# Second attention: the mask added by VectorE, scores in single-bank steps, and one fixed TensorE order of 270 steps

## The chip, the core and the metric

The kernel runs on one core of one Trainium2 chip. The metric is device time in microseconds (us), here that of this one core. TensorE multiplies matrices into banks of PSUM (a tile of this kernel takes one bank, 512 fp32 columns at most); VectorE (DVE in the rows) and ScalarE (ACT) read PSUM and work on SBUF; GpSimd (POOL) works on SBUF; DMA queues are issued from SyncE (SP) and GpSimd. Each engine runs its own list of instructions in order and waits on semaphores that others raise.

## The reference

Three stages run one after the other on 4 batches of 576 positions with 512 features:

```python
x = attn(q, k, v)            # 8 heads of 64; half local, half strided masks
x = moe(x, ...)              # 8 experts, one chosen per position
# second attention: 4 experts that are attention heads of 64, top 2 per position
for e in range(E):
    q, k, v = x @ wq[e], x @ wk[e], x @ wv[e]
    scores = scale * (q @ k.transpose(0, 2, 1))
    scores = np.where(causal, -1e9, scores)       # causal: key after query
    a = exp(scores - scores.max(-1)); a /= a.sum(-1) + 1e-9
    out += top2_weight(e) * (a @ v @ wo[e])
```

The change concerns the third stage alone.

## The kernel before, in words

The second attention holds, per batch, the 4 experts as two pairs (`pr` 0 and 1) of two heads (`h`). Its work is cut into steps, each a Python function that issues instructions for several engines:

- `c_load`/`c_t`: load 128 positions of the second stage's output and transpose them on TensorE; ScalarE and VectorE split the result into a high and a low part (`split`, L106 to L108).
- `c_qk`: 12 matmuls of 288 columns (tile `qkp`, three per product, `mm3` at L110 to L113); ScalarE and VectorE then make the halves of `qkt` (L1160, L1161 and `split`). `c_v`: 12 matmuls of 260 columns (`vp`).
- `c_s`: one **unit** of scores, that is one pair and one block `i` of queries (0 to 4; keys 64, 192, 320, 448 or 576). For blocks 0 and 1 both heads share one PSUM bank (tile `cs`), for 2 and 3 each head has one, for 4 each head has two of 288 keys. Of a pair's 10 banks 8 end on the diagonal, 64 in the stage. In such a bank a bf16 matmul against an identity (L1225, `idb` as weights, `mc` as data, 128 columns for one head, 2 x 64 or 2 x 128 for two) first writes the mask, then two fp32r matmuls per head add the scores (L1230). VectorE takes the row maximum (L1232), ScalarE the exponential and its sum (L1234), VectorE the reciprocal and weight (L1250 to L1252, or L1240 to L1247 for block 4), both engines scale the rows (L1257, L1259), and GpSimd clears 64 columns behind them (L1260). Tile `E` has 3 buffers; the banks of `cs` come in turn from three (`rot`, L95: two of tag `s`, one of `et`).
- `c_et`: transposes of one head's scaled scores (tile `cet`, two banks, L1274 and L1279), copied to SBUF by ScalarE or VectorE (L102, L104).
- `c_pv`: the product with the values for 256 or 320 queries (tile `cpv`, L1304): 4 or 10 matmuls in plain fp32, two records each. The two heads use the two halves of TensorE's columns.
- `c_out`: 6 matmuls of 512 columns (`cop`), a ScalarE copy and the DMA out.

`c_qk`, `c_v`, `c_pv`, `c_out` and, from batch 1 on, `c_t` take three banks in turn (`misc`, L96: `xt`, `lg`, `pv`).

Each step has a due time (tables `TAB`; a unit is 2 apart from the next), the steps are issued in the order of these times (L1382), and the framework's scheduler then sets every engine's list, moving instructions of different steps past and between each other. This is so for TensorE too: in the second attention nothing fixes its order by hand (the second stage does, `tc.manual_schedule`).

## Time and profile before

| what | value |
|---|---|
| median of 3 runs | 608.93 us (606.72 to 610.8) |
| the profiled execution: own time | 608.12 us |
| its span, first to last instruction | 606.3 us |
| TensorE busy, share of the span | 95% |
| VectorE, ScalarE, GpSimd | 61%, 58%, 24% |
| second attention on TensorE | first transpose at 386.96 us, last matmul at 601.39 us |

How to read it: matmuls are pipelined, so a matmul's duration in the rows (0.29 us for 288 columns) is longer than the time it costs in a row of such matmuls (0.13 us from start to start). What a matmul costs is therefore read here from the start of one to the start of the next. In the timeline rows, instructions of one line and shape that follow each other stand as one row with their count.

### The profile page before, as it was taken

How to read it: one execution, taken by the hardware profiler on the slowest of the kernel's cores; microseconds unless marked ns; L12 is line 12 of the kernel's file. 1: busy time of each engine (PE TensorE's matmuls, PEld its weight loads, DVE VectorE, ACT ScalarE, POOL GpSimd, SP SyncE). 2: the span in 40 equal slices, each digit the busy share in tenths (PEclk: the TensorE clock that was granted, in tenths of full speed). 3: DMA queues.
4: the chain of work that ended last, by engine and by line, in shares of the span. 5: the costliest groups of instructions: out<-in, count | busy, mean ns of one | idle time of the engine just before them, and what ended most of it. 6: DMA issues, size and time to landing. Idle time of an engine off the chain costs nothing. (4 is left out here: it accounts for less than half of the span.)

```text
span 606.3 us, 14268 instructions
## 1 busy us (share of the span) xinstructions
PE 578.4 (95%) x5329; PEld 493.5 (81%) x5329; DVE 371.8 (61%) x1071; ACT 349.9 (58%) x868; POOL 147.9 (24%) x229
## 2 busy tenths in 40 slices
PE   7898999889899999999999999999999999999996
PEld 4786788678688998989898977898888897988764
DVE  3456788936565563554646564358877686867671
ACT  2565767531555554445555665338677676847782
POOL 8242323421333423343343543200000000000000
PEclk9699799979999999999999999999999999999999
DMA  9999889440695472566566510424015102211202
GB/s 181 175 243 261 211 204 257 129 131 23 216 325 160 163 219 96 193 241 211 169 190 179 172 60 14 147 64 126 1 41 136 61 12 58 82 54 40 75 37 86
DMA packets 81219, 82.47 MB, mean 136 GB/s; under 512 B 56808, under 2 KB 56808, under 8 KB 80624
## 3 DMA queue, kind: packets, MB, share of 16 engines
q1 hardware_dynamic: 73024, 65.58, 39.0%
q0 software_dynamic: 8112, 15.76, 7.9%
q8 instruction: 55, 0.90, 0.6%
q14 instruction: 28, 0.23, 0.1%
HBM read 62.42 MB, written 21.76 MB: 139 GB/s over the span
## 5 line engine op out<-in xcount | busy, mean ns | idle before, releaser
L185 POOL DMA_INDIRECT yd<-y,sidx x47 | 54.1, 1150 | 81.9 <-ACT y L951 52.3
L108 DVE TENSOR_TENSOR w1l<-w1raw,w1h 128x1024 fp32r<-128x1024 f32 (+1 forms) x44 | 42.2, 982 | 30.5 <-ACT w1h L107 30.5
L1260 POOL MEMSET E<- 128x128 f32 x40 | 8.2, 207 | 188.4 <-PE cet L1279 93.9
L111 PE MATMUL yp<-w2h,h 128*128 128x512 f32 x128 | 52.8, 412 | 0.4 <-ACTq L961 0.4
L1234 ACT ACTIVATE E<-cs,c_mx 128x288 f32<-128x288 f32 (+4 forms) x96 | 45.9, 483 | 9.1 <-DVE c_mx L1232 4.8
L107 ACT ACTIVATE w1h<-w1raw 128x1024 fp32r<-128x1024 f32 (+1 forms) x44 | 34.4, 833 | 28.6 <-PE hp L113 18.5
L113 PE MATMUL yp<-w2h,h 128*128 128x512 f32 x128 | 50.3, 393 | 0.0
L112 PE MATMUL yp<-w2l,h 128*128 128x512 f32 x128 | 49.9, 390 | 0.0
L108 DVE TENSOR_TENSOR w2l<-w2raw,w2h 128x512 fp32r<-128x512 f32 x56 | 35.6, 684 | 11.6 <-ACT w2h L107 5.4
L1230 PE MATMUL cs<-qkt 128*128 128x288 f32 (+4 forms) x192 | 41.9, 331 | 0.0
L1232 DVE TENSOR_REDUCE c_mx<-cs 128x1 f32<-128x288 f32 (+4 forms) x80 | 37.8, 484 | 2.9 <-PE cs L1230 2.2
L111 PE MATMUL qkp<-y,cw 128*128 128x288 f32 x128 | 39.1, 305 | 0.4 <-DVE y L108 0.4
L113 PE MATMUL qkp<-y,cw 128*128 128x288 f32 x128 | 37.8, 296 | 0.0
L112 PE MATMUL qkp<-y,cw 128*128 128x288 f32 x128 | 37.8, 296 | 0.0
L107 ACT ACTIVATE w2h<-w2raw 128x512 fp32r<-128x512 f32 x56 | 32.3, 632 | 9.0 <-PE yp L113 4.5
L694 DVE SCALAR_TENSOR_TENSOR h<-hp,h 128x384 fp32r<-128x384 f32 x48 | 24.9, 550 | 14.5 <-ACT h L693 14.5
L951 ACT ACTIVATE y<-yp,pslot 128x512 f32<-128x512 f32 x22 | 14.9, 683 | 31.5 <-PE yp L113 22.9
L111 PE MATMUL hp<-xo,w1h 128*128 128x320 f32 (+1 forms) x96 | 31.7, 331 | 0.0
L179 POOL DMA_INDIRECT xg<-xd,gidx x24 | 24.4, 1016 | 27.8 <-DVE gidx L637 20.8
L111 PE MATMUL hp<-xh,w1h 128*128 128x384 f32 (+2 forms) x96 | 30.8, 321 | 0.0
L112 PE MATMUL hp<-xo,w1h 128*128 128x320 f32 (+1 forms) x96 | 30.6, 319 | 0.0
L113 PE MATMUL hp<-xo,w1l 128*128 128x320 f32 (+1 forms) x96 | 30.6, 318 | 0.0
(365 smaller groups left out, 1730.8 us busy)
## 6 DMA issues: line engine op xcount, KB each, us to landing
w1raw<-in_moe_w_dram SPq DMA_DIRECT2D x32, 512.0 KB
w2raw<-in_moe_w_dram SPq DMA_DIRECT2D x56, 256.0 KB
yr<-yd SPq DMA_DIRECT2D x20, 256.0 KB
qkt<-qkt SPq DMA_DIRECT2D x8, 576.0 KB
out_dram<-co SPq DMA_DIRECT2D x16, 256.0 KB
raw<-in_q_dram SPq DMA_DIRECT2D x16, 144.0 KB
raw<-in_k_dram SPq DMA_DIRECT2D x16, 144.0 KB
raw<-in_q_dram SPq DMA_DIRECT2D x8, 288.0 KB
```

The source lines that it names most:

```text
L107: nc.scalar.activation(hi, src, AF.Copy)
L108: (eng or nc.vector).tensor_tensor(lo, src, hi.bitcast(FT), op=OP.subtract)
L111: nc.tensor.matmul(o, ah, bh, start=start, stop=False, **kw)
L112: nc.tensor.matmul(o, ah, bl, start=False, stop=False, **kw)
L113: nc.tensor.matmul(o, al, bh, start=False, stop=stop, **kw)
L179: nc.gpsimd.indirect_dma_start(out=t, out_offset=None, in_=xd[:rows], in_offset=bass.IndirectOffsetOnAxis(ap=gidx[:, r, e:e + 1], axis=0))
L185: nc.gpsimd.indirect_dma_start(out=yds[n], out_offset=bass.IndirectOffsetOnAxis(ap=ix(n), axis=0), in_=y, in_offset=None, bounds_check=yds ...
L694: nc.vector.scalar_tensor_tensor(lo, p, 0.0, hi.bitcast(FT), op0=OP.max, op1=OP.subtract)
L951: nc.scalar.activation(y, p, AF.Copy, scale=pslot[:, r, e:e + 1])
L1230: nc.tensor.matmul(o[:, h - h0], T[:, h, q0:q0 + PQ], T[:, 2 + 2 * x + h, k0:k1], start=x == 0 and not last, stop=x == 1, skip_group_check ...
L1232: nc.vector.tensor_reduce(mx[:PQ, n, h0:h0 + G], o, axis=AX.X, op=OP.max, negate=True)
L1234: nc.scalar.activation(E[:PQ, h, k0:k1], o[:, h - h0], AF.Exp, bias=mx[:PQ, n, h:h + 1], accum_out=sm[:PQ, n, h:h + 1])
```

## The change

`c_s` is cut into one step for each PSUM bank of scores (`groups`); the mask matmul is gone, and in its place VectorE adds the bf16 mask `mc` in PSUM, onto the 128 (or 2 x 64, 2 x 128) diagonal columns of a finished bank, before it takes the maximum. Tiles, buffers, banks and all other instructions stay as they are, and so does the choice of engine for every copy. The 270 steps are sorted by due time as before, then put into the order of a table `ORD2`, and `manual_schedule` makes TensorE's list follow it; the lists of the other engines are still set by the scheduler.

```diff
+ORD2 = [0, 17, 7, 2, 3, 1, 8, 4, 6, 5, 9, 11, 10, 12, 13, 20, 14, 16, 15, 19, 18, 22, 24, 21, 26, 23, 30, 36, 27, 32,
...
-    def c_s(g):
+    def groups(i):
+        nk = NS[i + 1]
+        if nk <= 256:
+            return [(0, 0, nk, 0, 2)]
+        parts = [(0, nk)] if nk <= 512 else [(0, 288), (288, nk)]
+        return [(n, k0, k1, h, 1) for n, (k0, k1) in enumerate(parts) for h in range(2)]
+
+    def c_s(g, j):
...
+        n, k0, k1, h0, G = gs[j]
+        last = k1 == nk
+        p = cbank("cs", [128, G, 512 // G], "cs")
+        o = p[:, :, :k1 - k0]
+        for h in range(h0, h0 + G):
+            for x in range(2):
+                nc.tensor.matmul(o[:, h - h0], T[:, h, q0:q0 + 128], T[:, 2 + 2 * x + h, k0:k1],
+                                 start=x == 0, stop=x == 1, skip_group_check=True)
+        if last:
+            d = p[:, :, q0 - k0:k1 - k0]
+            nc.vector.tensor_tensor(d, d, mc[:, None, :P].to_broadcast([128, G, P]), op=OP.add)
+        nc.vector.tensor_reduce(mx[:, n, h0:h0 + G], o, axis=AX.X, op=OP.max, negate=True)
...
-                if last:
-                    nc.tensor.matmul(p[:PQ, :, q0 - k0:k1 - k0], idb[:PQ, :PQ],
-                                     mc[:PQ, None, :P].to_broadcast([PQ, G, P]), start=True, stop=False,
-                                     skip_group_check=True)
...
-    for _, f, a in sorted(ev, key=lambda x: x[0]):
+    ev.sort(key=lambda x: x[0])
+    cctx.enter_context(tc.manual_schedule(engines={mybir.EngineType.PE}))
+    for i in ORD2 or range(len(ev)):
+        _, f, a = ev[i]
         f(*a)
```

On TensorE, at the seam between batch 0 and batch 1 (`cpv` is the product with the values, `cs` the scores, `cet` the transposes, `qkp` and `cop` the projections). Before:

```order
L1304 MATMUL cpv<-et,vz_7194 64x320
L1230 MATMUL cs<-qkt 128x64 x4
L1230 MATMUL cs<-qkt 128x192 x4
L1304 MATMUL cpv<-et,vz_7194 64x320 x5
L1304 MATMUL cpv<-et,vz_7194 64x192 x2
L1304 MATMUL cpv<-et,vz_7194 64x64 x2
L1279 MATMUL cet<-idf,E 128x128
L1304 MATMUL cpv<-et,vz_7194 64x256
L1279 MATMUL cet<-idf,E 128x128
L1304 MATMUL cpv<-et,vz_7194 64x256
L1304 MATMUL cpv<-et,vz_7194 64x128 x2
```

The same two products after the change:

```order
L1241 MATMUL cs<-qkt 128x64 x4
L1297 MATMUL cet<-idf,E 128x128 x2
L1322 MATMUL cpv<-et,vz_7194 64x320 x6
L1322 MATMUL cpv<-et,vz_7194 64x192 x2
L1322 MATMUL cpv<-et,vz_7194 64x64 x2
L1241 MATMUL cs<-qkt 128x192 x4
```

```order
L1322 MATMUL cpv<-et,vz_7194 64x256 x2
L1322 MATMUL cpv<-et,vz_7194 64x128 x2
```

Each product with the values had been cut in two, its first matmul ahead of other work; now each runs in one piece (between the two pieces shown stand six matmuls of `cop`). Over the whole stage the 16 products stood in 23 pieces and now stand in 15, one of them two products long.

On TensorE, batch 0, pair 1, block 2. Before, with the mask's weights and matmul ahead of each head's scores:

```order
L1274 MATMUL cet<-idf,E 128x128
L1279 MATMUL cet<-idf,E 128x128
L1225 LDWEIGHTS idb
L1225 MATMUL cs<-mc,idb 128x128
L1230 MATMUL cs<-qkt 128x320 x2
L1225 LDWEIGHTS idb
L1225 MATMUL cs<-mc,idb 128x128
L1230 MATMUL cs<-qkt 128x320 x2
```

After the change the same block's scores, with those of block 0 behind them:

```order
L1241 MATMUL cs<-qkt 128x320 x4
L1241 MATMUL cs<-qkt 128x64 x4
L1292 MATMUL cet<-idf,E 128x128 x3
L1297 MATMUL cet<-idf,E 128x128
L1292 MATMUL cet<-idf,E 128x128 x3
L1297 MATMUL cet<-idf,E 128x128
```

All 64 mask matmuls with their weight loads are gone from TensorE's list (three of them had been moved ahead, into the end of the second stage).

On VectorE, at the last two units of the last batch (`c_mx` the maxima, `c_sm`, `c_rw` the sums and weights, `et` copies of transposes). Before:

```order
L1232 TENSOR_REDUCE c_mx<-cs 128x1
L108 TENSOR_TENSOR ot_9871<-cpv,ot_9870 128x256
L1252 TENSOR_TENSOR c_rw<-c_sm,t_w 128x2
L1232 TENSOR_REDUCE c_mx<-cs 128x1
L108 TENSOR_TENSOR ott<-cpv,ott 128x64
L1259 TENSOR_SCALAR E<-E,c_rw 128x448
L1232 TENSOR_REDUCE c_mx<-cs 128x1 x2
```

After:

```order
L1246 TENSOR_REDUCE c_mx<-cs 128x1
L1269 RECIPROCAL c_sm<-c_sm 128x2
L1245 TENSOR_TENSOR cs<-cs,mc 128x128
L1270 TENSOR_TENSOR c_rw<-c_sm,t_w 128x2
L1246 TENSOR_REDUCE c_mx<-cs 128x1
L1277 TENSOR_SCALAR E<-E,c_rw 128x448
L1245 TENSOR_TENSOR cs<-cs,mc 128x128
L1246 TENSOR_REDUCE c_mx<-cs 128x1
L119 TENSOR_TENSOR ot_9882<-cpv,ot_9881 128x256
```

Each of the 64 adds (L1245) stands ahead of its bank's maximum, with at most a few instructions of other steps between.

## Rows read from the trace of the kernel before

**Rows 1.** The page, clock granted to TensorE in 40 slices, tenths of full.

```profile
PEclk9699799979999999999999999999999999999999
```

**Rows 2.** Windows: length, busy us of PE, PEld, DVE, ACT, POOL, clock, DMA.

```profile
400.20:452.20 52.00, 50.46 (x395) 46.23 (x394) 41.45 (x156) 35.33 (x116) 1.90 (x9) 1.00 0.23 58
452.20:504.20 52.00, 51.37 (x381) 44.80 (x380) 37.78 (x137) 35.47 (x116) 2.05 (x10) 1.00 0.26 69
504.20:556.20 52.00, 52.00 (x383) 45.62 (x382) 36.54 (x135) 35.42 (x114) 1.85 (x9) 1.00 0.22 59
```

**Rows 3.** Groups by form, 391 to 606 us, mask matmuls: busy, mean ns.

```profile
L1225 PE MATMUL cs<-mc,idb 128*128 128x128 bf16 x54 | 12.2, 226 | 0.1
...
L1225 PE MATMUL cs<-mc,idb 128*128 128x256 bf16 x7 | 2.0, 279 | 0.0
```

**Rows 4.** Timeline of TensorE, block 2's scores: start us, length us, what, count.

```profile
441.37 0.22 PE L1225 MATMUL cs<-mc,idb 128*128 128x128 bf16 x1
...
441.78 0.23 PE L1225 MATMUL cs<-mc,idb 128*128 128x128 bf16 x1
...
442.19 0.29 PE L111 MATMUL qkp<-y,cw 128*128 128x288 f32 x1
442.32 0.29 PE L112 MATMUL qkp<-y,cw 128*128 128x288 f32 x1
```

**Rows 5.** Timeline of TensorE, a long product with the values in one piece.

```profile
432.09 0.27 PE L1279 MATMUL cet<-idf,E 128*128 128x128 f32 x1
432.29 2.28 PE L1304 MATMUL cpv<-et,vz 128*64 128x320 f32 x20
434.50 0.66 PE L1274 MATMUL cet<-idf,E 128*128 128x128 f32 x4
```

**Rows 6.** Timeline of TensorE, a short product in one piece.

```profile
576.97 0.87 PE L1304 MATMUL cpv<-et,vz 128*64 128x256 f32 x8
577.77 0.66 PE L1274 MATMUL cet<-idf,E 128*128 128x128 f32 x4
```

**Rows 7.** Timeline of TensorE, two products in two pieces each.

```profile
451.66 0.29 PE L113 MATMUL qkp<-y,cw 128*128 128x288 f32 x1
451.89 0.75 PE L1304 MATMUL cpv<-et,vz 128*64 128x320 f32 x2
452.57 1.14 PE L1230 MATMUL cs<-qkt 128*128 128x64 f32 x8
453.63 2.27 PE L1304 MATMUL cpv<-et,vz 128*64 128x320 f32 x18
455.83 0.33 PE L1279 MATMUL cet<-idf,E 128*128 128x128 f32 x1
456.09 0.65 PE L1304 MATMUL cpv<-et,vz 128*64 128x256 f32 x2
456.67 0.33 PE L1279 MATMUL cet<-idf,E 128*128 128x128 f32 x1
456.94 0.86 PE L1304 MATMUL cpv<-et,vz 128*64 128x256 f32 x6
457.74 0.40 PE L111 MATMUL qkp<-y,cw 128*128 128x288 f32 x1
```

**Rows 8.** Waits of TensorE, 391 to 606 us: total us, times, longest.

```profile
PE cet L1279 <- POOL E L1260: 1.3, 2, 0.6
PE cet L1279 <- DVE c_sm L1251: 1.0, 1, 1.0
```

**Rows 9.** Groups by form, VectorE, operations on a PSUM tile: busy, mean ns.

```profile
L108 DVE TENSOR_TENSOR ot<-cpv,ot 128x256 fp32r<-128x256 f32 x16 | 6.7, 420 | 7.7 <-ACT ot L107 7.7
...
L108 DVE TENSOR_TENSOR ott<-cpv,ott 128x64 fp32r<-128x64 f32 x8 | 1.7, 218 | 0.4 <-ACT ott L107 0.3
```

**Rows 10.** Timeline of TensorE, the last scores and their transposes.

```profile
586.66 0.51 PE L1230 MATMUL cs<-qkt 128*128 128x288 f32 x2
...
591.82 0.60 PE L1274 MATMUL cet<-idf,E 128*128 128x128 f32 x4
```

## The prediction

> **What bounds the kernel now.** I read the page first for the clock: TensorE had the full clock from the tenth of 40 slices on, all through the second attention [rows 1]; nothing is to be won or lost there unless long gaps appear. Then the windows view, cut at the repeating pattern of the batches, which is 52.0 us long: TensorE is busy 50.5, 51.4 and 52.0 of each 52 us; VectorE 41.5, 37.8 and 36.5; ScalarE 35 [rows 2]. So the stage is TensorE's, and its own list of instructions, not a wait for others, sets the time of a batch. Then the timeline of TensorE, from start to start, for what each kind of work costs it there; then its waits, for what is left over. The two longest groups of them in the stage, 2.3 us together, are three transposes of small units that wait for their scaled or cleared scores [rows 8].

> **Mask matmuls removed.** The mask's groups count 54 of 128 columns and 7 of 256 in the stage [rows 3]; the other 3 of the 64 ran in the end of the second stage, in gaps, and count nothing. From one mask's start to the next in block 2 is 0.41 us, and again 0.41 to the projection behind it [rows 4]. Each stretch holds one mask and two matmuls of 320 columns. A 288-column matmul costs 0.13 us (442.19 to 442.32) [rows 4], by columns 0.148 for 320, 0.296 for two. The mask is the rest, 0.115 us, about twice what 128 columns cost at that rate. (The row's mean of 226 ns [rows 3] is not it, since records overlap.) 61 x 0.115 = **7.0 us**, all on TensorE's path. Bounds: 4.0 us, if only columns counted (54 x 0.059 + 7 x 0.118, from the same 0.13), and 7.4 if the seven wide ones cost their further 128 columns on top (7 x 0.059). The stretch was measured, so I take its value.

> **Products with the values kept together.** A long product in one piece lies between the transpose that starts at 432.09 and the next at 434.50: 2.41 us, of which 0.11 is the transpose itself, so 2.3 [rows 5]. At the seam of batches 0 and 1 the first matmul of such a product stands apart: from the projection's start at 451.66 to the scores at 452.57 are 0.91 us, less its own 0.13 leaves 0.78; the other 18 records then still take 2.2 us (453.63 to 455.83) [rows 7]. One matmul less saves nothing there, because the two heads use the two halves of the array: alone, a matmul takes the time of a pair. The short product is the same: the six records that are left take 0.80 us (456.94 to 457.74) [rows 7], as do all eight in one piece (576.97 to 577.77) [rows 6], and the piece cut off costs 0.84 - 0.11 = 0.73 us (455.83 to 456.67) [rows 7]. The order shows 23 pieces for 16 products before, that is eight cuts: four of long products, three of short ones, and a fourth of a short one whose piece stands joined to the long product ahead of it. After the change no product is cut. 4 x 0.78 + 3 x 0.73, and half of 0.73 for the joined piece: **5.7 us**. Bounds: 4.5 (start to start of the pieces alone, 4 x 0.68 + 3 x 0.58, from 451.89 and 456.09 [rows 7]) and 6.2 (eight at 0.78).

> **Adds on VectorE.** No row shows an add onto scores in PSUM. The nearest are subtractions that read a PSUM tile: 218 ns for 64 columns, 420 ns for 256 [rows 9]; on the line between them 128 columns cost 285 ns. 48 single heads and 8 units of block 0 (2 x 64) at 285 ns, 8 of block 1 (2 x 128) at 420: 16.0 + 3.4 = 19.3 us, 4.8 us a batch. The ends are 14 us (all at 218) and 27 us (all at 420). On a batch VectorE then has 46.3, 42.6 and 41.4 us of work, against 52.0 - (16 x 0.115 + 2 x 0.75) = 48.7 us of TensorE's. It stays below, at 85% to 95%, so I cost the adds at nothing but for the waits below. Their cover is TensorE's own work, and in batch 0 it is thin; with it gone, an add costs its 0.285 us.

> **Waits.** An add stands ahead of its bank's maximum, and behind the maximum stand the exponential, the sums, the scaling, the transposes and the release of the bank; in VectorE's list it also stands ahead of copies that free TensorE's other banks. Two waits that I see go: the small units' transposes (2.3 us [rows 8]) now mostly have 4 to 7 us of TensorE work between their scores and them. New ones come, by the order at the rates above: the first units of the last batch have 3 to 4 us of work there, little for such a chain with an add in it (under 1 us together); the last unit's four banks stand back to back with three banks to take turns, so its last two wait for an add, a maximum and an exponential (1 to 1.5 us); and its transposes come some 4.6 us behind it, against 5.2 us from the start of the last scores before (586.66 to 591.82 [rows 10]), with a chain that is longer by an add or two (0.3 to 0.6 us). I put the new ones at 2.5 us, the old ones at 2.3: **0.2 us** lost, with -3 (no new waits, and smaller ones gone) and +7.4 (every second add, 9.7 us, on the path, less the 2.3) as the ends.

> **Moved steps.** A unit's banks of scores now stand apart, with projections and products between; the same matmuls, copies and weight loads are issued, and a step that is moved on TensorE takes its copies along in the scheduler's lists. The cover of the moved steps is distance: a bank of the `misc` three comes round again after about 2 us of TensorE work at the least. If VectorE is late by more than that leaves, rival 2 begins. On SP's queue the loads of the next batch are issued before steps that they followed, and each copy of `qkt` stands behind loads that wait for a transpose step; by the order some 5 us of TensorE work or more still lie between that transpose step and the first scores that need the copy. GpSimd's list keeps its memsets in the units' order. The tail is as before: three `c_out` steps of six matmuls behind the last product, a copy and the DMA. I cost all this at nothing.

> **Sum.** 608.1 (the profiled execution's own time) - 7.0 - 5.7 + 0.2 = **595.6 us**. The median of the runs shown, 608.9, is 0.8 above the profiled execution, well inside the range.

> **The rivals.**

> 1. *The waits go too.* The table orders all steps at once, where due times and the scheduler left the waits of the stage. For it: VectorE has slack in batches 1 and 2. Against it: the short distances in the last batch. With 5 us of them gone, 608.1 - 12.7 - 5 = 590 us. Chance 0.17.

> 2. *VectorE takes back part of it.* If every second add (9.7 us) ends up ahead of something that TensorE waits for, the time is 608.1 - 12.7 + 9.7 = 605; with a third of them, 602. For it: VectorE at 95% in batch 0, with ScalarE between its instructions. Against it: TensorE's waits before were 2.3 us while VectorE was busy for 80% in the same batch [rows 2, 8]. I take 604, just under the half. Chance 0.20.

> 3. *Slower: VectorE becomes the engine that sets the batch.* VectorE works in order, so an add that waits for late scores holds up the copies behind it; these hold the `misc` banks, TensorE comes later, the next scores too. The place is batch 0, where 41.5 us of work and 10.5 us idle make up the 52 us [rows 2]; it decides from the point where VectorE's idle time can't shrink below what its waits for ScalarE and TensorE need. With all idle time kept, every add counts: 608.1 - 12.7 + 19.3 = 615 us, and 622 with the upper price of 27. Against it: VectorE's load differs by 5 us between batches at one length of batch, so idle time is what gives. Chance 0.07.

> 4. *A mask matmul costs only its columns.* Then the masks give 4.0 us and not 7.0, and the time is 598.6. Against it: the stretch of 0.41 us [rows 4]. Chance 0.05. [...]

> That TensorE's list does not follow the table is no rival: the order shows no mask matmul and no cut product in it.

> **How the numbers follow.** My forecast has 0.51, with a range of its own from 592 to 600, by the bounds of the two gains and by waits between -3 and +4. The range for 8 in 10 takes in rivals 1 and 4 and most of 2: 589 to 604.5; it leaves out rival 3, the upper part of 2 and a little below. Faster by over 1% is below 602.8 us, and about 1% is what a measurement of this kernel can tell from no change: the forecast, rivals 1 and 4 and a quarter of 2 give 0.51 + 0.17 + 0.05 + 0.05 = 0.78. Within 1% (to 615 us): the rest of 2 and half of 3, 0.15 + 0.03 = 0.18. Slower: 0.04.

> **What would show it.** In the profile after: no mask row on TensorE, and score matmuls of 320 columns that start 0.30 us a pair; 15 pieces of value products, long ones of 2.3 us; a batch of 48 to 49 us, with TensorE busy for nearly all of it; VectorE at 42 to 46 us a batch, its adds at 0.22 to 0.42 us; the longest waits of TensorE in the last batch, for scaled scores and for banks of scores. I am wrong if a batch is still 51 us or more: then TensorE's new gaps, and the VectorE rows that end them, name rival 2 or 3. If the masks' stretches are 0.35 us, rival 4 holds.

## The result, and the profile after

The changed kernel takes 601.58 us in the median of 4 runs (601.08 to 603.35), the kernel before 609.87 us beside it (4 runs, 606.72 to 611.71): a ratio of 0.9875, 95% interval 0.9826 to 0.9923. So it is faster, by 8.3 us in the medians; 13.3 us were forecast. The profiled execution takes 601.53 us of its own time, 6.6 less than that of before.

The page's row of granted clock, changed kernel, has a new entry, the 8 in slice 28:

```profile
PEclk9699799999999999999999999998999999999999
```

The windows view, cut where the batches repeat (their first scores start at 404.33, 453.00, 503.52 and 553.52 us; columns as in [rows 2]):

```profile
404.33:453.00 48.67, 45.65 (x349) 43.01 (x347) 42.81 (x169) 33.52 (x112) 1.84 (x9) 0.96 0.21 53
453.00:503.52 50.52, 50.45 (x388) 44.63 (x387) 42.09 (x157) 36.29 (x119) 2.05 (x10) 1.00 0.26 72
503.52:553.52 50.00, 48.64 (x362) 44.49 (x363) 40.52 (x151) 36.56 (x116) 1.84 (x9) 1.00 0.23 62
```

A batch took 52.0 us before; now they take 48.7, 50.5 and 50.0, where 48 to 49 were forecast, and in two of them TensorE has 1.4 to 3.0 us without work.

No mask row is left on TensorE, and the value products are whole. The timeline of TensorE, a long and a short one (columns: start us, length us, what, count):

```profile
453.36 0.44 PE L1297 MATMUL cet<-idf,E 128*128 128x128 f32 x2
453.73 2.28 PE L1322 MATMUL cpv<-et,vz 128*64 128x320 f32 x20
455.93 0.69 PE L1241 MATMUL cs<-qkt 128*128 128x192 f32 x4
...
457.98 0.87 PE L1322 MATMUL cpv<-et,vz 128*64 128x256 f32 x8
458.78 0.40 PE L122 MATMUL qkp<-y,cw 128*128 128x288 f32 x1
```

From start to start the long one takes 2.20 us (453.73 to 455.93) and the short one 0.80, as in [rows 5, 6]; the pieces of [rows 7] are gone. The last long product alone is longer, 2.94 us, of which some 0.7 us is counted below as a wait. The adds, by groups and shape on VectorE (columns: busy us, mean ns, idle time before them):

```profile
L1245 DVE TENSOR_TENSOR cs<-cs,mc 128x128 f32<-128x128 f32 x56 | 15.7, 291 | 1.6 <-PE cs L1241 1.5
...
L1245 DVE TENSOR_TENSOR cs<-cs,mc 128x256 f32<-128x256 f32 x8 | 3.4, 421 | 0.0
```

They are the 19.1 us that were priced at 19.3 from [rows 9]. What is larger is the list of TensorE's waits over the second attention (columns: who waits for whom, us in total, times, longest), against [rows 8]:

```profile
PE cet L1292 <- ACT et L115: 2.1, 1, 2.1
PE cet L1292 <- DVE y L119: 1.3, 1, 1.3
PE cet L1292 <- ACT E L1275: 1.1, 2, 0.9
PE cs L1241 <- ACT E L1248: 0.9, 2, 0.7
```

**Where the time went.** I measured the stage from the first transposition of `yt` to the last matmul, since what lies ahead is the same code in all kernels and yet ends between 386.5 and 390.8 us, with spells of half clock that differ between the traces (10.2 us from 15.9 and 6.8 us from 60.2 and from 125.1 in that of before, the first two alone, from 15.7 and 60.0, in that of the change). Each matmul's end was compared with the end of the matmul ahead; what exceeds the median for that pair of kinds by over 60 ns is called a wait, and in stretches at a granted clock of 0.5 an excess under 0.4 us is put down to the clock. All in us:

| | before | after | difference | forecast |
|---|---|---|---|---|
| masks, scores, transposes, projections | 173.8 | 166.1 | -7.7 | -7.0 |
| products with the values | 32.7 | 27.2 | -5.5 | -5.7 |
| waits | 8.0 | 12.6 | +4.6 | +0.2 |
| half clock | 0 | 1.6 | +1.6 | 0 |
| stage | 214.6 | 207.6 | -7.0 | -12.5 |

The gains came; waits and clock took 6.2 us of them back. (The stage starts 0.4 us later, which makes the 6.6.)

The longest wait is in batch 0. TensorE's timeline, changed kernel (in brackets: idle time before, and who ended it):

```profile
411.86 0.38 PE L1297 MATMUL cet<-idf,E 128*128 128x128 f32 x2
412.08 0.60 PE L1047 MATMUL yt<-idf,yr 128*128 128x128 f32 x4
414.82 0.33 PE L1292 MATMUL cet<-idf,E 128*128 128x128 f32 x1 [2.14 <-ACT et L115]
```

The two `cet` at 411.86 are block 0's transposes. Those at 414.82 are block 1's, whose scores ended at 408.55; they need their own scaled scores and a bank that block 0's copy frees. ScalarE's timeline there:

```profile
411.74 0.42 ACT L1248 ACTIVATE E<-cs,c_mx 128x192 f32<-128x192 f32 x1 [1.18 <-DVE c_mx L1246]
...
413.78 0.44 ACT L1275 ACTIVATE E<-E,c_rw 128x192 f32<-128x192 f32 x1
414.25 0.40 ACT L118 ACTIVATE qkt<-qkp 64x288 fp32r<-64x288 f32 x1
414.56 0.20 ACT L115 ACTIVATE et<-cet 128x64 f32<-128x64 f32 x1
```

Block 1's exponential starts 3.2 us behind its scores, the scaling is done at 414.2, and block 0's copy stands behind all of it. Right behind the gap the clock falls. Windows of 3 us (columns as in [rows 2]):

```profile
412.00:415.00 3.00, 0.86 (x9) 0.62 (x7) 2.46 (x9) 2.95 (x12) 0.20 (x1) 1.00 0.37 93
415.00:418.00 3.00, 3.00 (x14) 2.81 (x14) 2.69 (x9) 1.11 (x5) 0.20 (x1) 0.50 0.00 0
```

TensorE had 0.86 us of work in the first window, and the granted clock is 0.50 in the second (from 415.0 to 418.4 in the trace's clock events).

### The profile page after: what moved, and what is told of

It is laid out like the page before. It is cut to its first block, busy times and chain, and to the rows that moved or that the text cites. A ratio compares the mean times of both kernels' runs of the same rounds, so it can differ in the third digit from the quotient of the medians.

```text
span 599.7 us, 14224 instructions
## 1 busy us (share of the span) xinstructions
PE 566.1 (94%) x5265; PEld 488.3 (81%) x5265; DVE 384.8 (64%) x1135; ACT 349.3 (58%) x868; POOL 147.8 (25%) x229
## 5 line engine op out<-in xcount | busy, mean ns | idle before, releaser
L1248 ACT ACTIVATE E<-cs,c_mx 128x288 f32<-128x288 f32 (+4 forms) x96 | 45.7, 481 | 17.1 <-DVE c_mx L1246 14.6
L1241 PE MATMUL cs<-qkt 128*128 128x288 f32 (+4 forms) x192 | 38.5, 319 | 1.1 <-ACT E L1248 0.9
L124 PE MATMUL qkp<-y,cw 128*128 128x288 f32 x128 | 37.8, 295 | 0.0
L1292 PE MATMUL cet<-idf,E 128*128 128x128 f32 x160 | 28.3, 279 | 5.0 <-ACT et L115 2.1
L122 PE MATMUL hp<-xo,w1h 128*128 128x320 f32 (+1 forms) x96 | 31.7, 331 | 0.0
L1241 PEld LDWEIGHTS cs<-qkt 128*128 128x128 f32 x192 | 28.7, 193 | 3.2 <-ACT E L1248 2.5
L190 POOL DMA_INDIRECT xg<-xd,gidx x24 | 24.4, 1017 | 26.1 <-DVE gidx L648 19.1
```

Of the source, the lines that this page charges most:

```text
L122: nc.tensor.matmul(o, ah, bh, start=start, stop=False, **kw)
L124: nc.tensor.matmul(o, al, bh, start=False, stop=stop, **kw)
L190: nc.gpsimd.indirect_dma_start(out=t, out_offset=None, in_=xd[:rows], in_offset=bass.IndirectOffsetOnAxis(ap=gidx[:, r, e:e + 1], axis=0))
L1241: nc.tensor.matmul(o[:, h - h0], T[:, h, q0:q0 + 128], T[:, 2 + 2 * x + h, k0:k1], start=x == 0, stop=x == 1, skip_group_check=True)
L1248: nc.scalar.activation(E[:, h, k0:k1], o[:, h - h0], AF.Exp, bias=mx[:, n, h:h + 1], accum_out=sm[:, n, h:h + 1])
L1292: nc.tensor.transpose(p[:, kt * 128:kt * 128 + 128], E[:, kt * 128:kt * 128 + 128], idf)
```

## The experiments

Two theories were set against each other at first. **A:** the adds make VectorE's list longer, so banks and transposed tiles come late. **B:** the waits belong to the fixed order, which leaves too little TensorE work between a step and its reader, whoever adds the mask. The first four runs shared one chip and 19 runs of the kernel before (610.08 us); so did each later group with its own.

**Order alone (e1_mask_on_tensore).** The changed kernel, mask on TensorE:

```diff
+        if last:
+            nc.tensor.matmul(p[:, :, q0 - k0:k1 - k0], idb, mc[:, None, :P].to_broadcast([128, G, P]),
+                             start=True, stop=False, skip_group_check=True)
...
-                                 start=x == 0, stop=x == 1, skip_group_check=True)
-        if last:
-            d = p[:, :, q0 - k0:k1 - k0]
-            nc.vector.tensor_tensor(d, d, mc[:, None, :P].to_broadcast([128, G, P]), op=OP.add)
+                                 start=x == 0 and not last, stop=x == 1, skip_group_check=True)
```

> The changed kernel with the mask back on TensorE (61 matmuls of the mask, no add on VectorE); steps and their order as in the changed kernel. The changed kernel's own profiled time is 601.5 us; of the 13.3 us forecast, 6.6 came, and from the first transposition of the second attention to its last matmul TensorE waits 12.6 us instead of 8.0 and runs at the half clock from 415.0 to 418.4 us, about 1.6 us. Theory A (the adds lengthen VectorE's in-order list, and banks and transposed tiles come late): the masks come back at 7.8 us, the value products stay whole, the waits fall by 3 to 5 us and the half clock at 415 goes: 602 to 605 us. Rival B (the waits come from the fixed order, whose distances between a step and its reader are too short whoever adds the mask): the waits stay at 12 to 13 us and the half clock stays: 608.5 to 610. VectorE's busy time falls by 19 us by both.

Measured: 609.99 us, ratio to before 0.9994 (0.9960 to 1.0028). The products with the values take 27.1 us, as in the changed kernel; the masks are back (scores and masks 33.8 us against 26.2: 7.6 us, 0.119 us each of 64); waits are 12.5 us and half clock 1.7. B holds. TensorE's timeline of this kernel has its longest gap in the same place:

```profile
414.93 0.37 PE L1292 MATMUL cet<-idf,E 128*128 128x128 f32 x1 [2.04 <-ACT et L115]
```

ScalarE's timeline there, this kernel:

```profile
411.60 0.42 ACT L1248 ACTIVATE E<-cs,c_mx 128x192 f32<-128x192 f32 x1 [1.12 <-DVE c_mx L1246]
...
414.67 0.20 ACT L115 ACTIVATE et<-cet 128x64 f32<-128x64 f32 x1
```

The exponential starts 0.14 us earlier than with the adds (this kernel's stage starts 0.15 us earlier too), and the copy comes 0.11 later: the same gap, with no add on VectorE.

The run leaves one thing open, and so do e3 and e4. TensorE's list in the stage is the same in all three as in the changed kernel, instruction for instruction (e1's masks apart). VectorE's and ScalarE's lists are not: the scheduler sets them anew for each kernel, and of VectorE's 550 other instructions at most 432 (e1), 434 (e3) and 453 (e4) stand in the changed kernel's order. So these runs price the adds together with the lists that the scheduler makes for them; adds in otherwise unchanged lists were not tried.

So the order by itself is worth nothing here: what whole products give (5.6 us) it gives back in waits and clock (4.5 + 1.7).

**Adds alone (e2_adds_scheduler_order).** The kernel before, mask on VectorE:

```diff
-                if last:
-                    nc.tensor.matmul(p[:PQ, :, q0 - k0:k1 - k0], idb[:PQ, :PQ],
-                                     mc[:PQ, None, :P].to_broadcast([PQ, G, P]), start=True, stop=False,
-                                     skip_group_check=True)
...
-                                         start=x == 0 and not last, stop=x == 1, skip_group_check=True)
+                                         start=x == 0, stop=x == 1, skip_group_check=True)
+                if last:
+                    d = p[:, :, q0 - k0:k1 - k0]
+                    nc.vector.tensor_tensor(d, d, mc[:, None, :P].to_broadcast([128, G, P]), op=OP.add)
```

> The kernel before with the mask added by VectorE and no other edit: scores as one step of a unit, and the scheduler's own order on TensorE (which may choose a somewhat different one, since the mask's matmuls are gone). Theory A (the adds make the waits, in any order): 609.9 - 7.8 for the masks + 3 to 5 of waits = 605 to 607 us, with value products still cut by other work. Rival B (the waits belong to the fixed order): 609.9 - 7.8 = 601 to 603 us, with TensorE's waits in the stage near the 8.0 us of before.

Measured: 613.97 us, ratio 1.0060 (1.0023 to 1.0097): slower. The masks' time is gone and the cuts are there (32.6 us), but the waits are 18.2 us, 10.2 more than before, more than either theory gave. The two longest groups of TensorE's waits in this kernel:

```profile
PE cet L1273 <- ACT qkt L1160: 2.5, 2, 1.6
PE cet L1278 <- POOL E L1259: 1.1, 1, 1.1
```

So the two parts do not add: order alone 0, adds alone +4, together -8 us. The scheduler, without masks to place, also chose other lists than before: at most 1344 of TensorE's 1467 other instructions and 408 of VectorE's 550 stand in the old order. Adds under the very order of before were not tried, so how much of the 10.2 us is the adds' and how much that choice's stays open.

**No mask (e3_no_mask).** The three lines of the add taken out:

```diff
-        if last:
-            d = p[:, :, q0 - k0:k1 - k0]
-            nc.vector.tensor_tensor(d, d, mc[:, None, :P].to_broadcast([128, G, P]), op=OP.add)
```

> The changed kernel without any mask: neither the adds on VectorE nor the matmuls; it leaves the mask out of the second attention's scores. Same steps and order. It prices all that the adds do to TensorE's waits. Theory A: the wait of 2.1 us at 412.7 us, the half clock behind it and most of the waits for banks in the last two units go: 595 to 597 us. Rival B (the fixed order makes the waits): 600.5 to 601.5 us, with the gap at 412.7 us still there.

Measured: 601.41 us (597.92 to 604.05), ratio 0.9826 (0.9757 to 0.9896); in the profile the stage takes 208.2 us against 207.6, with waits of 15.2 us and no half clock. TensorE's timeline of this kernel still has the gap in batch 0:

```profile
416.07 0.33 PE L1289 MATMUL cet<-idf,E 128*128 128x128 f32 x1 [1.47 <-ACT et L115]
```

The gap is 0.7 us shorter and the half clock is gone, as A had it, but other waits are longer by more. B again in the time: in this order the adds, with the lists that come with them, cost nothing that I can measure.

**Adds twice (e4_adds_twice).**

```diff
             nc.vector.tensor_tensor(d, d, mc[:, None, :P].to_broadcast([128, G, P]), op=OP.add)
+            nc.vector.tensor_tensor(d, d, mc[:, None, :P].to_broadcast([128, G, P]), op=OP.add)
```

> The changed kernel with every add of the mask issued twice: 64 more adds, 19.1 us more of VectorE (the mask is added twice, which changes nothing in what is kept). Theory A (VectorE's list is close to setting the pace): at 180 us of work in some 207 us of stage, 5 to 12 us more: 607 to 614 us, with TensorE's waits grown by as much. Rival B (VectorE has room, the order makes the waits): under 2 us more: 601.5 to 603.5.

Measured: 616.22 us, ratio 1.0105 (1.0018 to 1.0192). This is above the 607 to 614 that A gave, and far above B. The stage takes 221.7 us, 14.1 more, for 64 further adds; waits are 25.3 us and half clock 2.8. So A has its place too, but further out. One row of the windows view over the whole stage (the fourth figure behind the bounds is VectorE's busy time), first with no mask (e3):

```profile
389.24:597.70 208.46, 199.52 (x1469) 175.19 (x1467) 150.84 (x550) 143.71 (x462) 9.75 (x43) 1.00 0.23 64
```

The same row of the changed kernel, adds once:

```profile
387.32:595.15 207.83, 200.43 (x1469) 177.38 (x1467) 163.24 (x614) 143.58 (x462) 9.79 (x43) 0.99 0.23 64
```

And with adds twice (e4):

```profile
387.45:609.37 221.92, 204.77 (x1469) 177.81 (x1467) 176.65 (x678) 144.66 (x462) 9.96 (x43) 0.98 0.22 60
```

The 19.1 us of adds are the sum of their records, and records overlap: VectorE's busy time grows by only 12.4 us for the first 64 adds and by 13.4 for the second. It goes from 72% to 79% busy for nothing, and from there the stage grows by as much as VectorE's work (14.1 us, the clock included). VectorE's idle time in the stage tells the same: 57.6 us with no mask, 44.6 with the adds once, 45.3 with the adds twice. The first adds were paid out of idle time, the second were not. So the changed kernel stands near the end of what idle time gives, as far as two points and lists set anew can tell, and a share of 79% did not mean that a fifth was free.

**Filling gaps (e5_first_gap, e6_three_gaps).** The next runs move steps of the table; `s` is a step of scores, `et` one of transposes, `t` one of `yt`, `qk` one of queries and keys. In e5 four steps stand ahead of block 1's `et`:

```diff
-ORD2 = [..., 16, 15, 19, 18, 22, 24, 21, 26, 23, 30, 36, ...
+ORD2 = [..., 16, 15, 19, 18, 21, 26, 23, 30, 22, 24, 36, ...
```

> The changed kernel with four steps of its fixed order moved: scores of block 2 head 1 and of block 3 head 0 and two transpositions of y stand ahead of the transpositions of block 1 in batch 0, 1.6 us of TensorE's work put into the gap of 2.1 us at 412.7 us; nothing else. Theory B (the distances of the fixed order make the waits; the run without adds had the gap too): the gap falls to 0.5-1 us, and with it the half clock behind it goes (1.6 us): 598.5 to 600 us of the profiled run, if its time before the stage is as in the changed kernel (387.3 us to the first transposition). Theory A' (VectorE and ScalarE are behind by then, whatever TensorE does meanwhile): the wait moves to the steps after, and 601 to 602 stays; the half clock goes only if the gap does.

Measured: 601.27 us, ratio 0.9835 (0.9792 to 0.9878); stage 206.6 us, waits 13.2, no half clock. The gap did not fall, it moved into the steps put in front, as TensorE's timeline of e5 shows:

```profile
414.23 0.63 PE L1048 MATMUL yt<-idf,yr 128*128 128x128 f32 x4 [1.09 <-issue]
...
416.32 0.63 PE L1048 MATMUL yt<-idf,yr 128*128 128x128 f32 x4 [1.46 <-DVE qkt L120]
```

`t` takes turns in the three `misc` banks, and those still held queries and keys that ScalarE and VectorE had not split. Only the clock's 1.6 us came back. e6 does the same at two more gaps (`qk` ahead of block 2's `et`, scores and a `t` ahead of block 1's in batch 2):

```diff
-67, 68, 70, 72, 71, 75, ...    152, 158, 157, 153, 154, 165, ...
+67, 68, 70, 75, 72, 71, ...    152, 158, 153, 154, 165, 157, ...
```

> As the run before, and two more gaps filled: the fourth step of queries and keys ahead of block 2's transpositions (gap of 0.9 us at 449.8 us) and block 2's scores and a transposition of y ahead of block 1's of batch 2 (gap of 1.3 us at 508.7 us). Theory B: 1.5 to 2 us less than with the first gap alone, 597 to 598.5 us. Theory A': as with the first gap alone, since what is moved away is missing later as cover.

Measured: 602.97 us, ratio 0.9877 (0.9826 to 0.9928); stage 207.8, waits 14.6: the gap of 0.9 us at 449.8 came back as three of 0.8, 0.9 and 0.5 us at 450 to 453, the one of 1.3 stands ahead of the `t`. As A' said.

**Copies to ScalarE (e7, and e8 with e6's order).**

```diff
-EE = ["avava", "vavav"]
-VE = "ava" "va"
+EE = ["avava", "vavaa"]
+VE = "aaa" "aa"
```

> The changed kernel with 16 kinds of copy moved from VectorE to ScalarE: head 1's transposed tiles of block 4 and the values' copies of two of five blocks; VectorE loses some 9 us, ScalarE gains as much; the order is the same. Theory A' (VectorE is too full): 2 to 4 us less, 598 to 600. Theory B (the waits are latencies of chains through both engines in a fixed order): within 1 us of the changed kernel, or slower, since the copies that TensorE waits for at 412.7 are ScalarE's.

> The three filled gaps and the copies on ScalarE together. If both help by themselves and add: 595 to 597 us. If the waits only move: 600 to 602.

Measured: 603.52 us, ratio 0.9856 (0.9809 to 0.9903), and 603.16 us, 0.9872 (0.9823 to 0.9920); stages of 209.3 and 210.7 us. The changed kernel's row over the stage again, for e7 (the fifth figure is ScalarE's busy time):

```profile
387.72:597.26 209.54, 200.49 (x1469) 177.33 (x1467) 156.76 (x590) 151.08 (x486) 9.87 (x43) 0.99 0.23 64
```

In all 24 copies moved. VectorE's busy time fell from 163.2 to 156.8 us, ScalarE's rose from 143.6 to 151.1, and the stage grew by 1.7. So these waits do not hang on VectorE's share alone; what less work on VectorE would give with no more on ScalarE, this run can't tell.

**The order itself (e9_plain_order).**

```diff
-ORD2 = [0, 17, 7, 2, 3, ...
+ORD2 = []
```

> The changed kernel with its table of the order left empty: the same 270 whole steps, adds on VectorE, in the order of the due times that the kernel before gave to the scheduler as priorities. It tells what the order chosen is worth beside whole steps alone. Value products stay in one piece by all theories (15 or 16 of them, about 27 us). If whole steps in any order do it: 600 to 604 us. If the chosen order takes up waits that a plain one has: TensorE's waits in the stage 20 us or more instead of 12.6, and 609 to 625 us.

Measured: 654.07 us, ratio 1.0757 (1.0695 to 1.0819), far above even the 609 to 625 expected. The products stay whole (28.2 us), the waits are 53.9 us and half clock 8.5. The longest group of its waits, one that neither kernel's list shows:

```profile
PE cs L1231 <- DMA qkt<-qkt: 16.9, 3, 6.0
```

Three times scores stand too close behind the copy of `qkt` that SP's queue brings. So whole steps in a plain order bring 54 us more of waits and half clock than before, and the chosen order leaves 6 of them.

**Transposes earlier (e10_early_tiles).** Block 0's `et` ahead of the last `qk`, two `s` ahead of block 1's `et`:

```diff
-ORD2 = [..., 14, 16, 15, 19, 18, 22, 24, 21, 26, 23, ...
+ORD2 = [..., 14, 15, 19, 16, 18, 21, 26, 22, 24, 23, ...
```

> The changed kernel with block 0's transpositions of batch 0 moved ahead of the last step of queries and keys before them (1.8 us earlier, so that their copies are listed ahead of the exponentials), and two steps of scores ahead of block 1's transpositions; unlike the first-gap run no transposition of y, which there waited for a bank. If the gap at 412.7 is the copies that stand late in ScalarE's list: gap under 1 us, no half clock, 598.5 to 600 in the profile. If VectorE is behind whatever the order: as the first-gap run, 600 to 601, with 2 us or more of waits between 409 and 417 us.

Measured: 602.03 us, ratio 0.9872 (0.9839 to 0.9905); profile 599.3 us, the shortest stage of all, 205.9 us; waits 12.7, no half clock. The windows view of e10 where the changed kernel had its gap:

```profile
412.00:415.00 3.00, 1.93 (x14) 1.31 (x12) 2.35 (x10) 2.92 (x11) 0.20 (x1) 1.00 0.33 87
415.00:418.00 3.00, 1.93 (x17) 1.96 (x18) 2.94 (x10) 2.48 (x8) 0.00 (x0) 1.00 0.74 182
```

Block 1's wait is 1.00 us instead of 2.14, and the next `t` waits 1.15: the same 2.15 us in two parts, and the full clock. The profiled time lies in the range of the first case, the waits are those of the second, and the median shows no gain.

**The other engines' lists (e11_lists_by_program).**

```diff
-    cctx.enter_context(tc.manual_schedule(engines={mybir.EngineType.PE}))
+    cctx.enter_context(tc.manual_schedule(engines={mybir.EngineType.PE, mybir.EngineType.DVE,
+                                                   mybir.EngineType.Activation}))
...
```

(The rest of the edit takes the scaling out of `c_s` into a function that is called later, as told next.)

> The changed kernel with VectorE's and ScalarE's lists also fixed by hand: each step's work in the order of TensorE's steps, the scaling of a unit two steps behind its last scores (or just ahead of its transpositions). The same instructions on every engine. If the waits come from lists that the scheduler ordered by its own estimate (copies that free a bank behind splits that wait for TensorE): the waits fall, 595 to 600 us. If the scheduler's lists are better than program order: 605 us and more. If the lists' order does not matter: 601 to 603.

Measured: 689.44 us, ratio 1.1325 (1.1270 to 1.1379); waits 80 us, led by copies on ScalarE that stand behind work which is not ready, in the list of this kernel's waits:

```profile
PE cet L1295 <- ACT et L115: 35.5, 12, 8.2
```

So the order in VectorE's and ScalarE's lists matters as much as TensorE's, and the scheduler's lists are far better than program order.

**Two more gaps (e12_early_more).** Against e10 in batch 0, against the changed kernel in batch 2:

```diff
-..., 23, 30, 36, 27, 32, 25, ...    152, 158, 157, 153, 154, 165, ...
+..., 23, 27, 32, 30, 36, 25, ...    152, 158, 153, 154, 157, 165, ...
```

> The early-tiles kernel (its stage from the first transposition to the last matmul took 205.9 us, 1.6 less than the changed kernel's 207.6) with four more steps moved: two steps of scores ahead of the transposition of y that waited 1.15 us at 415-416, and block 2's scores ahead of block 1's transpositions in batch 2 (gap of 1.3 us), without the transposition of y that in the three-gaps run waited in its place. If a gap closes where work that waits for nothing is put in it: each of the two gaps falls by 0.5 to 0.7 us, the stage takes 204.5 to 205.2 us. If VectorE and ScalarE set the pace there: 205.7 to 206.5, the wait moved on. No half clock in the stage by either; the median near 600 to 602, since the time before the stage spreads by 2 to 3 us.

Measured: 604.12 us, ratio 0.9900 (0.9857 to 0.9942); stage 207.1, waits 13.8. The gap in batch 2 fell from 1.31 to 0.72 us, as put; in batch 0 the scores that were moved up waited 1.9 us for a bank, the longest of a group in this kernel's waits:

```profile
PE cs L1242 <- ACT E L1249: 2.7, 3, 1.9
```

No run beats the changed kernel beyond doubt: e5 and e10 have the better stage by 0.9 and 1.6 us in the one execution profiled of each, and medians that agree with its own within their spread.

## Why the prediction was right in direction and 6 us short

**The gains** were sized rightly. The row with the masks fell by 7.7 us for 7.0 forecast; with one order on both sides (e1 against the change) a mask costs 0.119 us, as the stretch of 0.41 us [rows 4] had said with 0.115. So rival 4 falls. The cuts gave 5.5 us for 5.7: a piece cut off a two-headed product costs its full 0.7 to 0.8 us [rows 7], and mending it returns that.

**The adds** were priced rightly as single instructions (291 and 421 ns for 285 and 420), and "at nothing but for the waits" holds in this order: no mask at all gives no shorter stage. As load on VectorE they were priced too high. The prediction set the mask's mean of 226 ns aside because records overlap, but took the adds' price from such means; VectorE's busy time grew by 12.4 us (e3 to the change), not 19.3, and batch 0 has 42.8 us of it in 48.7, 88% and not 95%. Rival 3, VectorE setting the batch, has its sign in e4: idle time no longer gives (45.3 us against 44.6), and the stage grows by the whole of the further work (14.1 us for 13.4). The change is not slowed by it, but stands close to that point.

**The waits** are the step that failed: +0.2 us forecast, +6.2 measured with the clock. What the prediction let go did go: neither group of [rows 8] stands in the changed kernel's list. But it said that the small units' transposes "now mostly have 4 to 7 us of TensorE work between their scores and them", took that for enough, and put new waits in batches 0 to 2 at nothing. The three longest waits of the changed kernel are there, ahead of transposes of block 1 (batches 0 and 2) and block 2 (batch 0). The first is shown above; TensorE's timeline at the other two:

```profile
444.59 1.11 PE L1241 MATMUL cs<-qkt 128*128 128x320 f32 x8
...
449.52 0.29 PE L124 MATMUL qkp<-y,cw 128*128 128x288 f32 x1
450.69 0.44 PE L1292 MATMUL cet<-idf,E 128*128 128x128 f32 x2 [0.88 <-ACT E L1275]
```

```profile
503.52 1.12 PE L1241 MATMUL cs<-qkt 128*128 128x64 f32 x8
...
508.05 0.60 PE L1047 MATMUL yt<-idf,yr 128*128 128x128 f32 x4
509.96 0.33 PE L1292 MATMUL cet<-idf,E 128*128 128x128 f32 x1 [1.31 <-DVE y L119]
```

The scores of the three units end at 408.55, 445.34 and 504.64 us (the second inside the row of eight, which goes on with block 0's scores), TensorE runs out of work at 412.68, 449.81 and 508.65, and the transposes start at 414.82, 450.69 and 509.96. So there were 4.1, 4.5 and 4.0 us of work, and the chain took 6.3, 5.4 and 5.3 us. The distance was read rightly and the chain taken as shorter than it is: maximum, two exponentials, sums, scaling, and the copy of the tile ahead that frees the bank, all in lists where splits of other tiles stand between. The 5.2 us from the start of the last scores to their transposes [rows 10] had shown such a chain with no add in it; I used it for the last unit only.

How far more distance would have helped is not shown. Steps put into a gap shortened it in batch 2, from 1.31 to 0.72 us (e12), though that stage was no shorter than e10's; in batch 0 the wait only moved on (e5, e6, e10). There ScalarE is busy for 2.95 and VectorE for 2.46 of the 3 us around the gap, so the work of these two engines may set the pace of that stretch whatever TensorE's order is. No run separates the two.

New waits were looked for in the last batch alone, where TensorE waits 4.7 us (2.5 of new ones forecast); batches 0 to 2 have 6.6 us where before had 3.7, and the half clock.

**The rival that came nearest in time is not borne out in its cause.** Rival 2 gave 602 us for a third of the adds on the path. Had the experiments stopped at the time, it would have passed. Without one add on VectorE the same TensorE order waits as much (e1, e3), though not at every place: the gap of 0.9 us at 449.8 is in neither. The time came back in waits that this order has with the adds or without them. And 601.6 us lies outside the forecast's own 592 to 600; the stated 589 to 604.5 holds it by the share of rival 2, so that the range was right is in part luck.

**What stays open:** why the kernel with the adds waits some 10 us more in the scheduler's order and no longer in the fixed one. In both comparisons VectorE's and ScalarE's lists changed along with the adds, and e9 and e11 show only that the orders of these lists and of TensorE's matter by tens of microseconds.

## What to carry to other kernels

Where a change has two parts, run each alone: here one is worth nothing, the other costs 4 us, and together they gain 8. Whether a fixed order will wait is read by setting the work between a step and its reader against the measured length of the chain on the other engines, with the release of the bank in it (here 4.0 to 4.5 us against 5.3 to 6.3); a gap that was filled by steps which need the same engines' banks only moved (e5: 2.14 us became 1.09 and 1.46). An engine's load is read from its busy time and not from the sum of its records (12.4 us against 19.1 for the adds), and a run that takes instructions away also gets new lists wherever a scheduler sets them. And a gap that costs TensorE its clock may be worth splitting even if its length cannot be shortened (e10 kept the full clock with 1.00 and 1.15 us; it did not help in e8, with 1.08 and 1.46).

## What the runs showed of the hardware

```profile
589.19 0.41 PE L1293 MATMUL cet<-idf,E 128*128 128x128 f32 x2 [0.70 <-DVE et L113]
591.42 1.78 PE L1241 MATMUL cs<-qkt 128*128 128x288 f32 x6 [1.12 <-ACT E L1249]
```

So the length of a gap alone does not tell. It cost 1.6 us in the change, 1.7 in e1 and 2.8 for the two in e4.

A mask matmul with its weight load, between others, cost 0.119 us in the mean of 64, 56 of them of 128 columns and 8 of 256 (e1 against the change), and one cut-off piece of a two-headed product 0.7 to 0.8 us [rows 7]. On VectorE 64 adds whose records sum to 19.1 us made 12.4 us of busy time (e3 to the change).
